# Chunked attention and its feed-forward layer on one core: paired chunks' attention parked in HBM, scale and bias applied to results, differences on VectorE, weight blocks stored later

## The chip, the core and the metric

The program runs on one core of a Trainium2 chip. The core has five engines with a queue each: TensorE (PE, matmuls; its weight loads are shown as PEld), VectorE (DVE), ScalarE (ACT), GpSimd (POOL) and SyncE (SP), whose queue issues every DMA here. The metric is device microseconds of one execution. Three runs of the kernel before gave 628.95, 630.91 and 631.41 us; the median is 630.91 us.

## The reference, cut to what matters

```python
# attention: batch 4, 8 heads, 768 positions, 64 per head; chunks of 32 queries
k_full = concat([mem_k, k[c_start-16 : c_end+8]]);  v_full likewise
scores = 0.125 * q_c @ k_full.T
a = exp(scores - max(scores));  a = a / (sum(a) + 1e-9)
out[c] = a @ v_full
# feed-forward on x = attention as 3072 tokens x 512
h = x @ w_in                     # 512 -> 2048
r = maximum(h, 0)
g = s * (r * r) + b              # s and b are two numbers
y = g @ w_out                    # 2048 -> 512, fp32
```

Since s and b are scalars, `g @ w_out` equals `s * ((r*r) @ w_out) + b * (column sums of w_out)`.

## The kernel before

The 3072 tokens are 8 chunks of 384 (`TOK`). Chunks 0 to 3 take the plain way, chunks 4 to 7 are taken in two pairs, (4,5) and (6,7). fp32 accuracy comes from splitting each operand in a high and a low fp32r part and adding three products.

Plain way: 64 steps, one for each block f of 128 hidden units of a chunk. `hidden` (L572) makes 12 matmuls of 384 columns; ScalarE applies relu, square, scale and bias and writes the high part gH (L580 to L583); VectorE writes the low part gL (L584); `result` (L595) makes 9 matmuls of 512 columns.

Attention comes in 32 visits, four for each chunk, two heads in each (`attend`). A visit is 16 score matmuls (L426), a maximum on VectorE (L494), exponentials on ScalarE (L498), a norm on GpSimd (L507, L510), 8 transposes on VectorE (L530) and 16 value matmuls (L465). For chunks 4 to 7 its result is copied to the ring `words` (L470): four tiles, which the weight loads and the weight blocks use as well.

Weights arrive as 64-bit numbers. 32 of them are put together by ScalarE and VectorE (L547 to L557), and for the pairs `blocks` makes sums of their quarters on GpSimd (L627 to L637), cuts these (L640, L641) and stores the blocks to HBM (L646): 48 stores of 256 KB come from weights as they are (`w1s<-w`, `w2s<-w`), 128 of 128 KB from sums (`<-words`).

A pair uses a seven-product scheme over 2 by 2 blocks. `mix` makes four differences of the attention's blocks on GpSimd (L707) and cuts seven operands (L702, L703). `seven` makes the hidden layer in 8 groups of 42 matmuls (L753), and on each group ScalarE does relu (L785), GpSimd the square (L787) and ScalarE scale and bias (L788). `rest` makes the second layer with 336 matmuls (L855), first taking 32 differences of hidden blocks on GpSimd (L800) and cutting 56 operands (L848 on ScalarE, L849 on VectorE). Weight blocks come back through SP (L731, `word`).

The order on all five engines is laid out when the program is built, by `Plan.lay`: a list planner with a cost for each kind of operation (`HOLD`), a due time for each (`anchor`, `base`), rings with a number of tiles, and a flag `lock` that keeps certain VectorE and GpSimd operations apart in the plan. On the chip each engine then runs its list in order.

Of the kernel before, what the change touches and what calls it, by code (L numbers as in the profile page):

```python
# [11 lines left out]
F32 = mybir.dt.float32  # L12
# [20 lines left out]
TOK = 384  # L33
GB = TOK // QB
# [18 lines left out]
LAST_VISITS = (0.5, 2.6)  # L53
# [19 lines left out]
            low=475, affine_v=475, rec=120, max=212, flip=449, xlow=470, wlow=345, wjoin=610, wsign=612, out=600,  # L73
            small=240, prod=1062, half=527, gsum=1000, add=480, wide=850, square2=1600, vsum=1230, ssum=620, shigh=930, slow=1143, tsum=1700, thigh=670, tlow=880, norm=1010, norm2=2030, wrest=1290, issue=440)
LATE = dict(PE=230, ACT=180, DVE=180, POOL=150, SP=0)
RATE, LAND = 400.0, 2000.0
# [65 lines left out]
class Plan:  # L142
# [25 lines left out]
    def lay(self, filler=None):  # L168
# [18 lines left out]
        while todo:  # L187
# [6 lines left out]
            for e in engines:  # L194
# [78 lines left out]
def body(ctx: ExitStack, tc: tile.TileContext, qkv, w1, w2, out):  # L273
# [3 lines left out]
    w2s = [dram.tile([P, 2, 2, 2 * P], F32, name=f"w2s{i}") for i in range(NWORDS)]  # L277
    plan = Plan()
# [38 lines left out]
    gs = Ring([(const.tile([P, TOK], F32R, name=f"gH{i}"), const.tile([P, TOK], F32R, name=f"gL{i}")) for i in range(3)])  # L317
# [78 lines left out]
    x_vals, open_ = {}, []  # L396

    def attend(ch, c):
# [166 lines left out]
    def hidden(u):  # L565
# [17 lines left out]
        op("ACT", "high", u - ahead, lambda: nc.scalar.activation(g.tile[0], hp(), AF.Copy), (h[0],), (g["H"],))  # L583
        op("DVE", "low", u - ahead, lambda: nc.vector.tensor_tensor(g.tile[1], hp(), g.tile[0].bitcast(F32), ALU.subtract),  # L584
# [35 lines left out]
    def blocks(side, g, due):  # L620
# [22 lines left out]
        for n, name in enumerate(BLOCKS):  # L643
# [8 lines left out]
            else:  # L652
# [3 lines left out]
                put(lambda i=i, k=k: weight_tile(side, fs[i])[:, :, k * 2 * P:(k + 1) * 2 * P].bitcast(F32), dst, parts[i], 0)  # L656
# [20 lines left out]
    cuts = Ring(Lazy([lambda k=k: gs.tiles[k] for k in range(3)] + [lambda s=s: (lambda x: (x[:, 0], x[:, 1]))(again(*s, [P, 2, TOK], F32R)()) for s in spots]))  # L677
# [12 lines left out]
    def mix(ch):  # L690

        due = base(ch) - 6.0
        raw = {name: x_vals[ch + int(name[2]) - 1, int(name[1]) - 1] for name in ("B11", "B12", "B21", "B22")}
        flat = lambda v: v.tile[:, :2 * TOK] if v.ring is words else v.tile.rearrange("p c t -> p (c t)")
        both = lambda v: [v[0], v[1]] if v.ring is words else [v[0]]
# [10 lines left out]
        def subtract(dst, a, b, prio):  # L706
            op("POOL", "tsum", due + prio, lambda: nc.gpsimd.tensor_tensor(flat(dst), flat(a), flat(b), ALU.subtract), [*both(a), *both(b)],  # L707
# [28 lines left out]
    def seven(ch, g):  # L736
# [46 lines left out]
        for v in (gb, ga):  # L783
# [3 lines left out]
            op("POOL", "square2", then, lambda v=v: nc.gpsimd.tensor_tensor(v.tile, v.tile, v.tile, ALU.mult), (), (v[0], v[1]), lock=True)  # L787
            op("ACT", "wide", then, lambda v=v: nc.scalar.activation(v.tile, v.tile, AF.Identity, scale=s_sb, bias=b_sb),  # L788
               (c_s[0], c_b[0]), (v[0], v[1]))

    def rest(ch):

        begin = base(ch) + NF // 2 * GROUP
        here, names = {}, ("P1", "P5", "P2", "P6", "P7", "P3", "P4")
        raw = lambda name, g: (gv[ch + int(name[2]) - 1, g], int(name[1]) - 1)
# [3 lines left out]
        def change(dst, a, b, due):  # L799
            op("POOL", "gsum", due, lambda: nc.gpsimd.tensor_tensor(at(dst), at(a), at(b), ALU.subtract), [part(a), part(b)], [part(dst)], lock=True)  # L800
            return dst

        def operand(name, g, due):
            if name == "P1":
                return raw("B11", g)
            if name == "P5":
                here["T1", g] = change(raw("B11", g), raw("B12", g), raw("B11", g), due - 2.0)
                return here["T1", g]
            if name == "P2":
                return raw("B21", g)  # L810
# [153 lines left out]
```

## Time and profile before

| | before |
|---|---|
| median of 3 runs | 630.91 us |
| the profiled execution | 629.65 us, of which the span is 627.9 us |
| TensorE busy | 602.2 us, 96% |
| VectorE busy | 458.3 us, 73% |
| ScalarE busy | 439.2 us, 70% |
| GpSimd busy | 309.6 us, 49% |
| HBM read, written | 98.57 MB, 35.65 MB |

Busy shares are means over stages with different limits, so they are read by stretch: start-up to about 20 us; weights arrive and are put together until about 121 us; plain steps with attention until about 355 us; the first pair until about 502 us (its `rest` begins at 427 us); the second pair until 624 us; then the last store.

### The profile page before, as it was taken

How to read it: one execution, taken by the hardware profiler on the slowest of the kernel's cores; microseconds unless marked ns; L12 is line 12 of the kernel's file. 1: busy time of each engine (PE TensorE's matmuls, PEld its weight loads, DVE VectorE, ACT ScalarE, POOL GpSimd, SP SyncE). 2: the span in 40 equal slices, each digit the busy share in tenths (PEclk: the TensorE clock that was granted, in tenths of full speed). 3: DMA queues.
4: the chain of work that ended last, by engine and by line, in shares of the span. 5: the costliest groups of instructions: out<-in, count | busy, mean ns of one | idle time of the engine just before them, and what ended most of it. 6: DMA issues, size and time to landing. Idle time of an engine off the chain costs nothing. (4 is left out here: it accounts for less than half of the span.)

```text
span 627.9 us, 11538 instructions
## 1 busy us (share of the span) xinstructions
PE 602.2 (96%) x3822; PEld 539.3 (86%) x3822; DVE 458.3 (73%) x1221; ACT 439.2 (70%) x1127; POOL 309.6 (49%) x290
## 2 busy tenths in 40 slices
PE   9999978999999999999999999999987999999997
PEld 5777867788888888798888999999877899999897
DVE  5999998954767687946777377678997844438874
ACT  6999997867778678659876667888752446656442
POOL 4522100384565687961234065765890526649710
PEclk9999998999999999999999999999997999999999
DMA  9977998425444546345337188777573787777671
GB/s 340 405 269 230 324 355 306 165 72 181 165 160 164 181 150 214 111 150 195 93 98 252 49 273 268 271 259 265 200 234 122 253 286 256 245 255 244 232 256 51
DMA packets 65531, 134.97 MB, mean 215 GB/s; under 512 B 6592, under 2 KB 37312, under 8 KB 65472
## 3 DMA queue, kind: packets, MB, share of 16 engines
q1 hardware_dynamic: 65472, 134.25, 62.7%
q8 instruction: 30, 0.49, 0.3%
q14 instruction: 29, 0.24, 0.1%
HBM read 98.57 MB, written 35.65 MB: 214 GB/s over the span
## 5 line engine op out<-in xcount | busy, mean ns | idle before, releaser
L572 PE MATMUL ps<-x,w 128*128 128x384 f32 x768 | 147.5, 339 | 1.7 <-DVE w L557 1.7
L572 PEld LDWEIGHTS ps<-x,w 128*128 128x128 f32 x768 | 134.8, 188 | 9.6 <-DVE w L557 3.1
L595 PE MATMUL ps<-w,gH 128*128 128x512 f32 x384 | 121.1, 397 | 0.0
L753 PE MATMUL ps<-again,again 128*128 128x384 f32 x672 | 120.3, 338 | 0.0
L753 PEld LDWEIGHTS ps<-again,again 128*128 128x128 f32 x672 | 117.8, 188 | 1.1
L498 ACT ACTIVATE t<-t,nmax 96x128 f32<-96x128 f32 x256 | 99.4, 392 | 18.1 <-DVE nmax L494 18.0
L530 DVE STREAM_TRANSPOSE aT<-t 32x256 f32<-32x256 f32 x192 | 83.6, 435 | 14.3 <-POOL t L510 11.7
L510 POOL TENSOR_TENSOR t<-t,rden 96x1024 f32<-96x1024 f32 (+1 forms) x40 | 66.8, 1672 | 52.8 <-DVE rden L509 52.7
L595 PE MATMUL ps<-w,gL 128*128 128x512 f32 x192 | 79.3, 413 | 9.9 <-DVE gL L584 9.8
L595 PEld LDWEIGHTS ps<-w,gH 128*128 128x128 f32 x384 | 72.8, 190 | 14.4 <-DVE w L557 0.6
L507 POOL TENSOR_SCALAR rden<-den 96x8 f32<-96x8 f32 (+1 forms) x40 | 13.2, 331 | 135.4 <-ACT t L498 134.4
L855 PE MATMUL ps<-gH,again 128*128 128x384 f32 x272 | 69.8, 337 | 0.0
L584 DVE TENSOR_TENSOR gL<-ps,gH 128x384 fp32r<-128x384 f32 x64 | 35.3, 552 | 46.2 <-ACT gH L583 45.6
L494 DVE CUSTOM_DVE_ANT_0 t<-ps,mask 96x128 f32<-96x128 f32 x256 | 57.8, 280 | 9.7 <-PE ps L426 9.4
L580 ACT ACTIVATE ps<-ps 128x384 f32<-128x384 f32 x64 | 30.4, 475 | 43.2 <-PE ps L572 43.1
L595 PEld LDWEIGHTS ps<-w,gL 128*128 128x128 f32 x192 | 36.4, 190 | 21.0 <-DVE gL L584 13.9
L855 PE MATMUL ps<-again,again 128*128 128x384 f32 x264 | 53.1, 348 | 0.0
L855 PE MATMUL ps<-gL,again 128*128 128x384 f32 x136 | 46.9, 345 | 3.6 <-DVE gL L849 3.5
L855 PEld LDWEIGHTS ps<-gH,again 128*128 128x128 f32 x272 | 49.5, 188 | 0.0
L855 PEld LDWEIGHTS ps<-again,again 128*128 128x128 f32 x264 | 47.8, 194 | 1.3 <-DVE again L849 0.8
L498 ACT ACTIVATION_READ_ACCUMULATOR t<-t,nmax 96x1 f32 x256 | 48.6, 190 | 0.0
L627 POOL TENSOR_TENSOR words<-w 128x512 f32<-128x512 f32 x32 | 45.4, 1438 | 0.7
(95 smaller groups left out, 1018.3 us busy)
## 6 DMA issues: line engine op xcount, KB each, us to landing
again<-w1s SPq DMA_DIRECT2D x56, 512.0 KB, 4.2
again<-w2s SPq DMA_DIRECT2D x56, 512.0 KB, 4.2
raw<-qkv SPq DMA_DIRECT2D x28, 448.0 KB, 4.0
words<-w SPq DMA_DIRECT2D x22, 512.0 KB, 5.2
w1s<-words SPq DMA_DIRECT2D x64, 128.0 KB, 1.9
w2s<-words SPq DMA_DIRECT2D x64, 128.0 KB, 1.9
v<-qkv SPq DMA_DIRECT2D x28, 256.0 KB, 3.7
w1s<-w SPq DMA_DIRECT2D x24, 256.0 KB, 4.3
```

What stands on the lines that cost most here:

```text
L494: op("DVE", "max", a + 0.1, lambda j=j: nc.vector.tensor_tensor_reduce(t.tile[:, n, j, :], scv()[:, j, :], mask[:, kind(j)], -SCALE, 3.0e3 ...
L498: op("ACT", "exp", a + 0.2, lambda j=j: nc.scalar.activation(t.tile[:, n, j, :], t.tile[:, n, j, :], AF.Exp, bias=nmax()[:, j:j + 1], scal ...
L507: op("POOL", "small", a + 0.25, lambda: nc.gpsimd.tensor_scalar(rden(), den(), 1e-9, None, ALU.add), [st["d", *x] for x in each], (r,), lo ...
L510: op("POOL", "norm2" if wide else "norm", a + 0.25, lambda: nc.gpsimd.tensor_tensor(t.tile[:, heads], t.tile[:, heads], rden().unsqueeze(3 ...
L530: nc.vector.transpose(aT.tile[gg, :, :, cs], t.tile[cs, :, :, gg])
L572: nc.tensor.matmul(h.tile[:, :TOK], weight_tile(0, f)[:, wi, c * P:(c + 1) * P], x.tile[c][:, xi], start=(c == 0 and n == 0), stop=(c == N ...
L580: op("ACT", "relu", u - ahead, lambda: nc.scalar.activation(hp(), hp(), AF.Relu), (), (h[0],))
L584: op("DVE", "low", u - ahead, lambda: nc.vector.tensor_tensor(g.tile[1], hp(), g.tile[0].bitcast(F32), ALU.subtract), (h[0], g["H"]), (g[" ...
L595: nc.tensor.matmul(acc.tile, g.tile[gi][:, t * P:(t + 1) * P], weight_tile(1, f)[:, wi, :], start=(first and n == 0), stop=(last and n == 2))
L627: op("POOL", "vsum", due, lambda k=k, f=f: nc.gpsimd.tensor_tensor(at(full, 2 * k, 2), weight_tile(side, f)[:, 0].bitcast(F32), weight_til ...
L753: nc.tensor.matmul(bank.tile[:, :TOK], w.tile[:, lo:lo + P], xv.tile[xi][:, kc], start=(not more and kc == 0 and i == 0), stop=(kc == 1 an ...
L855: nc.tensor.matmul(sb(bank), w.tile[:, lo:lo + P], cut.tile[xi], start=(first and k == 0), stop=(last and k == 2), skip_group_check=True)
```

## The change

Five edits. The attention of chunks 4 to 7 is copied to a small tile of another ring and stored to HBM (`xs`, 16 stores of 192 KB); `mix` loads it from there in 8 loads of 384 KB. So visits need no tile of `words`, and their due times run on at one spacing instead of a separate spacing for the last two chunks. In `mix` the differences are taken by VectorE, in `rest` too, except the first eight of each pair, which GpSimd takes right after the group that they need. In `seven` the square moves from GpSimd to ScalarE in the place of scale and bias; s and b act in `rest` on results: the cut operands get two columns more (386), ones in the high part and zeros in the low, so that column 384 of the bank holds the column sums, which ScalarE multiplies by b (`colsum`), and joins multiply by s. The 48 stores of plain weight blocks wait for the last weight (`all_w`). The planner's costs are changed and it knows a delay within one engine (`SAME`).

```diff
 HOLD = dict(...
-            small=240, prod=1062, half=527, gsum=1000, add=480, wide=850, square2=1600, ...
+            small=300, prod=1062, half=525, gsum=985, gsumv=470, tsumv=850, one=180, chigh=420, scaled=400, add=480, wide=735, ...
+SAME = dict(PE=0, ACT=118, DVE=115, POOL=60, SP=0)
...
-        last = (NCHUNK - 2 - NALONE) * (H // 2)
-        if ch < NCHUNK - 2:
-            return VISITS[0] + VISITS[1] * i
-        return base(NCHUNK - 4) + LAST_VISITS[0] + LAST_VISITS[1] * (i - last)
+        return VISITS[0] + VISITS[1] * i
...
-        x = x_vals[ch] if ch < NPLAIN else x_vals[ch, c // 2]
+        x = x_vals[ch] if ch < NPLAIN else Val(wvs, "st")
...
-                op("ACT", "xhigh", due + 0.9, lambda: nc.scalar.activation(x.tile[:, c % 2 * TOK:(c % 2 + 1) * TOK], av(), AF.Copy),
-                   (va[0],), (x[c % 2],))
+                op("ACT", "xhigh", due + 0.9, lambda: nc.scalar.activation(x.tile[:, :TOK], av(), AF.Copy), (va[0],), (x[0],))
+                op("SP", "issue", due + 0.9, lambda: nc.sync.dma_start(xs[ch, c // 2][:, c % 2], x.tile[:, :TOK]), (x[0],),
+                   (c_xs[ch, c // 2][c % 2],), size=P * TOK * 4)
...
-                put(lambda i=i, k=k: weight_tile(side, fs[i])..., dst, parts[i], 0)
+                put(lambda i=i, k=k: weight_tile(side, fs[i])..., dst, [*parts[i], *all_w], 0)
...
-        due = base(ch) - 6.0
+        due = base(ch) - 8.0
+        for name in ("B11", "B12", "B21", "B22"):
+            v, key = Val(words), (ch + int(name[2]) - 1, int(name[1]) - 1)
+            op("SP", "issue", due - 2, lambda v=v, key=key: nc.sync.dma_start(flat(v), xs[key].rearrange("p c t -> p (c t)")), ...)
...
-            op("POOL", "tsum", due + prio, lambda: nc.gpsimd.tensor_tensor(flat(dst), flat(a), flat(b), ALU.subtract), ...
+            op("DVE", "tsumv", due + prio, lambda: nc.vector.tensor_tensor(flat(dst), flat(a), flat(b), ALU.subtract), ...
...
-            op("POOL", "square2", then, lambda v=v: nc.gpsimd.tensor_tensor(v.tile, v.tile, v.tile, ALU.mult), (), (v[0], v[1]), lock=True)
-            op("ACT", "wide", then, lambda v=v: nc.scalar.activation(v.tile, v.tile, AF.Identity, scale=s_sb, bias=b_sb), ...
+            op("ACT", "wide", then, lambda v=v: nc.scalar.activation(v.tile, v.tile, AF.Square), (), (v[0], v[1]))
+        op("POOL", "gsum", then + 1, lambda: nc.gpsimd.tensor_tensor(gb.tile[:, 0], gb.tile[:, 0], ga.tile[:, 0], ALU.subtract), ...)
...
+            if name == "P6":
+                return change("DVE", t1, b22, t1, due - 2.0)
+            if name == "P7":
+                return change("DVE", b11, t1, b11, due - 2.0)
+            if name == "P4":
+                return change("DVE", b21, b21, t1, due - 2.0)
...
+        def colsum(i, bank, due):
+            op("ACT", "one", due, lambda: nc.scalar.activation(col(i), bank.tile[:, TOK:TOK + 1], AF.Identity, scale=b_sb), ...)
+        def join(dst, bank, v, due):
+            op("DVE", "add", due, lambda: nc.vector.scalar_tensor_tensor(sb(dst), sb(bank), s_sb, sb(v), ALU.mult, ALU.add), ...)
...
-                        nc.tensor.matmul(sb(bank), w.tile[:, lo:lo + P], cut.tile[xi], ...
+                        nc.tensor.matmul(sx(bank), w.tile[:, lo:lo + P], cut.tile[xi], ...
```

The first place is the queue of SP while weights arrive. `words<-w` is a weight load, `w1s<-w` and `w2s<-w` are stores of plain weight blocks. Before, a piece of the queue:

```order
L646 DMA w1s_71<-w_8_1051 128x2x256
L646 DMA w1s_73<-w_8_1051 128x2x256
L646 DMA w2s_94<-w_7_1064 128x2x256
L646 DMA w2s_110<-w_7_1064 128x2x256
L545 DMA words_155<-w 128x1024
L545 DMA words_152<-w 128x1024
L646 DMA w1s_74<-w_9_1107 128x2x256
L545 DMA words_153<-w 128x1024
L646 DMA w2s_87<-w_8_1121 128x2x256
L646 DMA w1s_74<-w_10_1132 128x2x256
L646 DMA w1s_76<-w_10_1132 128x2x256
```

Now, the end of the weight loads:

```order
L544 DMA words_160<-w 128x1024
L544 DMA words_161<-w 128x1024
L544 DMA words_162<-w 128x1024
L544 DMA words_163<-w 128x1024
L544 DMA words_160<-w 128x1024
L544 DMA words_161<-w 128x1024
L645 DMA w1s_57<-w_0_468 128x2x256
L645 DMA w1s_59<-w_0_468 128x2x256
L645 DMA w1s_60<-w_1_539 128x2x256
```

All 48 of these stores stood ahead of or among the last weight loads; now all 48 stand behind the last load.

The second place is VectorE in the `rest` of the first pair. `L849` and `L860` are the low cuts, `L530` transposes of a visit, `L835` joins, `L703` and `L707` cuts of the next pair's operands, `L803` a difference. Before:

```order
L849 TENSOR_TENSOR again_7_4242<-againx_3_4229,again_7_4242 128x384
L849 TENSOR_TENSOR gL_171<-again_14_4332,gH_170 128x384
L849 TENSOR_TENSOR gL_173<-again_15_4414,gH_172 128x384
L849 TENSOR_TENSOR gL_175<-againx_0_3753,gH_174 128x384
L530 STREAM_TRANSPOSE aT_163<-t_159 32x8x32 x6
L835 TENSOR_TENSOR wv_150<-ps_179,wv_150 128x384
L835 TENSOR_TENSOR wv_149<-ps_179,wv_149 128x384
L835 TENSOR_TENSOR wv_147<-ps_180,wv_147 128x384
L835 TENSOR_TENSOR wv_148<-ps_180,wv_148 128x384
L530 STREAM_TRANSPOSE aT_163<-t_159 32x8x32 x2
L849 TENSOR_TENSOR again_7_4156<-againx_2_3845,again_7_4156 128x384
```

Now:

```order
L860 TENSOR_TENSOR again_7_4431<-againx_0_3960,again_7_4431 128x384
L860 TENSOR_TENSOR gL_179<-againx_2_4084,gH_178 128x384
L803 TENSOR_TENSOR again_12_4180<-again_12_4161,again_12_4180 128x384
L860 TENSOR_TENSOR gL_181<-again_12_4161,gH_180 128x384
L707 TENSOR_TENSOR again_6_3714<-words_161,again_6_3713 128x768
L860 TENSOR_TENSOR gL_183<-again_13_4265,gH_182 128x384
L803 TENSOR_TENSOR again_13_4277<-again_13_4265,again_13_4277 128x384
L860 TENSOR_TENSOR again_7_4335<-againx_0_4376,again_7_4335 128x384
L803 TENSOR_TENSOR againx_1_4388<-againx_0_4376,againx_1_4388 128x384
L860 TENSOR_TENSOR again_7_4431<-againx_2_4450,again_7_4431 128x384
L803 TENSOR_TENSOR againx_3_4462<-againx_2_4450,againx_3_4462 128x384
```

Transposes and maxima of attention have left this stretch, differences have come in, one for each cut in the last three of the seven products. On TensorE the visits whose values came in the first pair's hidden layer and `rest` (8) become 6, all of them within the hidden layer.

## Rows read from the trace of the kernel before

**Rows 1.** The page's busy times: us, share of the span, instructions.
```profile
PE 602.2 (96%) x3822; PEld 539.3 (86%) x3822; DVE 458.3 (73%) x1221; ACT 439.2 (70%) x1127; POOL 309.6 (49%) x290
```

**Rows 2.** Waits of TensorE: us in all, times, the longest.
```profile
PE ps L595 <- DVE gL L584: 9.8, 7, 3.4
PE ps L465 <- DVE aT L530: 5.5, 3, 4.1
PE ps L855 <- DVE gL L849: 3.5, 3, 1.4
```

**Rows 3.** Stretches: length; PE, PEld, DVE, ACT, POOL busy (instructions); PEclk, DMA share, GB/s.
```profile
20.00:60.00 40.00, 38.74 (x302) 30.42 (x301) 38.37 (x127) 39.67 (x122) 14.92 (x16) 1.00 0.80 285
60.00:120.00 60.00, 51.41 (x265) 43.25 (x266) 55.34 (x118) 50.80 (x111) 2.84 (x5) 0.97 0.91 311
120.00:280.00 160.00, 157.66 (x979) 137.84 (x978) 112.14 (x319) 116.68 (x315) 112.36 (x116) 1.00 0.45 151
280.00:360.00 80.00, 79.74 (x544) 69.88 (x543) 50.89 (x165) 57.85 (x164) 20.23 (x16) 1.00 0.42 140
440.00:500.00 60.00, 52.03 (x316) 48.65 (x315) 53.18 (x112) 32.06 (x82) 38.64 (x28) 0.94 0.60 201
564.00:590.00 26.00, 25.09 (x137) 23.40 (x136) 22.73 (x24) 14.63 (x28) 21.93 (x18) 1.00 0.66 228
```

**Rows 4.** Three shorter stretches, same columns.
```profile
98.00:104.00 6.00, 3.35 (x8) 2.68 (x9) 4.13 (x8) 5.90 (x12) 0.00 (x0) 0.72 0.97 358
460.00:470.00 10.00, 8.72 (x46) 7.52 (x44) 9.74 (x8) 4.60 (x9) 10.00 (x8) 1.00 0.69 226
470.00:480.00 10.00, 5.89 (x29) 5.67 (x30) 7.84 (x16) 1.57 (x3) 2.33 (x3) 0.66 0.28 97
```

**Rows 5.** DMA issues from 28 to 121 us: KB each, median us to landing.
```profile
words<-w SPq DMA_DIRECT2D x18, 512.0 KB, 5.1
w1s<-w SPq DMA_DIRECT2D x23, 256.0 KB, 4.3
w2s<-w SPq DMA_DIRECT2D x22, 256.0 KB, 3.8
```

**Rows 6.** ScalarE's wait for weight loads, 70 to 120 us.
```profile
ACT wv L547 <- DMA words<-w: 4.3, 4, 2.9
```

**Rows 7.** VectorE from 441 to 476 us: start, us, operation.
```profile
441.21 3.58 DVE L530 STREAM_TRANSPOSE aT<-t 32x256 f32<-32x256 f32 x8
...
461.89 5.41 DVE L849 TENSOR_TENSOR gL<-again,gH 128x384 fp32r<-128x384 f32 x2
...
468.51 2.68 DVE L530 STREAM_TRANSPOSE aT<-t 32x256 f32<-32x256 f32 x6
...
475.04 0.55 DVE L849 TENSOR_TENSOR gL<-again,gH 128x384 fp32r<-128x384 f32 x1
```

**Rows 8.** All cuts of `rest` (L849): VectorE's busy time (instructions).
```profile
0.00:628.00 628.00, 85.15 (x112) 0.99 0.63 215
```

**Rows 9.** Groups by line: busy us, mean ns, idle before.
```profile
L494 DVE CUSTOM_DVE_ANT_0 t<-ps,mask 96x128 f32<-96x128 f32 x256 | 57.8, 280 | 9.7 <-PE ps L426 9.4
L703 DVE TENSOR_TENSOR again<-words,again 128x768 fp32r<-128x768 f32 x14 | 19.7, 1420 | 1.7 <-ACT again L702 1.5
L785 ACT ACTIVATE again<-again 128x768 f32<-128x768 f32 x8 | 6.8, 845 | 6.4 <-DVE again L779 6.4
L788 ACT ACTIVATE again<-again,b_sb,s_sb 128x768 f32<-128x768 f32 x16 | 16.4, 1026 | 5.4 <-POOL again L787 5.3
```

**Rows 10.** A cut of `mix` alone, and one beside GpSimd.
```profile
480.56 0.95 DVE L703 TENSOR_TENSOR again<-words,again 128x768 fp32r<-128x768 f32 x1
493.16 2.61 DVE L703 TENSOR_TENSOR again<-words,again 128x768 fp32r<-128x768 f32 x1
```

**Rows 11.** GpSimd's norm, by form.
```profile
L510 POOL TENSOR_TENSOR t<-t,rden 96x1024 f32<-96x1024 f32 x24 | 47.9, 1994 | 39.9 <-DVE rden L509 39.8
```

**Rows 12.** TensorE from 520 to 560 us, by line.
```profile
L753 PE MATMUL ps<-again,again 128*128 128x384 f32 x229 | 40.4, 337 | 0.0
```

More of the change, by code (lines that the diff above doesn't have):

```diff
@@ L72 @@
             relu=388, square=388, affine=570, high=388, xhigh=388, wscale=571, whigh=536, copy=270, exp=386, keep=388, store=480, bias=500,
[L73 to L74 removed]
+            low=475, affine_v=475, rec=120, max=212, flip=449, xlow=470, wlow=365, wjoin=610, wsign=612, out=600,
+            small=300, prod=1062, half=525, gsum=985, gsumv=470, tsumv=850, one=180, chigh=420, scaled=400, add=480, wide=735, vsum=1260, ssum=700, shigh=950, slow=1143, tsum=1800, thigh=735, tlow=880, norm=1010, norm2=1870, wrest=1290, issue=440)
 LATE = dict(PE=230, ACT=180, DVE=180, POOL=150, SP=0)
+SAME = dict(PE=0, ACT=118, DVE=115, POOL=60, SP=0)
 RATE, LAND = 400.0, 2000.0
@@ L253, in lay @@
                     d.left -= 1
-                    d.ready = max(d.ready, free[e] if d.eng == e and not o.size else o.end)
+                    d.ready = max(d.ready, free[e] + SAME[e] if d.eng == e and not o.size else o.end)
                     if not d.left:
@@ L277, in body @@
     w2s = [dram.tile([P, 2, 2, 2 * P], F32, name=f"w2s{i}") for i in range(NWORDS)]
+    xs = {(ch, i): dram.tile([P, 2, TOK], F32, name=f"xs{ch}_{i}") for ch in range(NPLAIN, NCHUNK) for i in range(NC_T // 2)}
     plan = Plan()
@@ L396, in body @@
     x_vals, open_ = {}, []
+    c_xs = {key: fixed() for key in xs}
     def attend(ch, c):
@@ L676, in body @@
     spots = [(0, 7), (1, 7)]
-    cuts = Ring(Lazy([lambda k=k: gs.tiles[k] for k in range(3)] + [lambda s=s: (lambda x: (x[:, 0], x[:, 1]))(again(*s, [P, 2, TOK], F32R)()) for s in spots]))
+    cuts = Ring(Lazy([lambda k=k: gs.tiles[k] for k in range(3)] + [lambda s=s: (lambda x: (x[:, 0], x[:, 1]))(again(*s, [P, 2, TOKX], F32R)()) for s in spots]))
     streams, stream_slots = later([(k, f) for f in range(8, 12) for k in range(2)], [P, 2 * DM], F32R)
@@ L801, in change @@
             return dst
         def operand(name, g, due):
[L804 to L810, printed above, removed]
+            b11, b21, t1, b22 = (gv[ch, g], 0), (gv[ch, g], 1), (gv[ch + 1, g], 0), (gv[ch + 1, g], 1)
             if name == "P6":
-                here["T2", g] = change(here["T1", g], raw("B22", g), here["T1", g], due - 2.0)
-                return here["T2", g]
+                return change("DVE", t1, b22, t1, due - 2.0)
@@ L847, in rest @@
                 gone = first("cut", [(4, k) for k in range(3)] + spots)
-                op("ACT", "high", due - AHEAD, lambda cut=cut, v=v: nc.scalar.activation(cut.tile[0], at(v), AF.Copy), (part(v),), [cut["H"], *gone])
-                op("DVE", "low", due - AHEAD, lambda cut=cut, v=v: nc.vector.tensor_tensor(cut.tile[1], at(v), cut.tile[0].bitcast(F32), ALU.subtract),
-                   (part(v), cut["H"]), [cut["L"], *gone], lock=True)
+                op("ACT", "chigh", due - AHEAD, lambda cut=cut, v=v: nc.scalar.activation(cut.tile[0][:, :TOK], at(v), AF.Copy), (part(v),), [cut["H"], *gone])
+                op("DVE", "low", due - AHEAD, lambda cut=cut, v=v: nc.vector.tensor_tensor(
+                    cut.tile[1][:, :TOK], at(v), cut.tile[0][:, :TOK].bitcast(F32), ALU.subtract), (part(v), cut["H"]), [cut["L"], *gone], lock=True)
+                ends = []
+                if gone:
+                    for k in range(2):
+                        ends.append(cut["end", k])
+                        op("ACT", "one", due - AHEAD - 1, lambda cut=cut, k=k: nc.scalar.activation(
+                            cut.tile[k][:, TOK:], ones[:, :TOKX - TOK], AF.Copy, scale=1.0 - k), (), [ends[k], *gone])
                 def products(bank, m, w, cut, first, last, q):
@@ L854, in products @@
                         lo = q * DM + wi * 2 * P + m * P
-                        nc.tensor.matmul(sb(bank), w.tile[:, lo:lo + P], cut.tile[xi], start=(first and k == 0), stop=(last and k == 2),
+                        nc.tensor.matmul(sx(bank), w.tile[:, lo:lo + P], cut.tile[xi], start=(first and k == 0), stop=(last and k == 2),
                                          skip_group_check=True)
@@ L859, in rest @@
                     op("PE", "half", due, lambda m=m, w=w, cut=cut, g=g, i=i, bank=banks_[m], more=more: products(
-                        bank, m, w, cut, g == 0 and not more, g == NF // 2 - 1, i % 2), (w[0], cut["H"], cut["L"]), (banks_[m][0],))
+                        bank, m, w, cut, g == 0 and not more, g == NF // 2 - 1, i % 2), (w[0], cut["H"], cut["L"], *ends), (banks_[m][0],))
             due -= AHEAD
@@ L912, in body @@
         result(u)
+    for ch in range(NPLAIN, NCHUNK):
+        visits(ch)
     for ch in range(NPLAIN, NCHUNK, 2):
-        visits(ch)
-        visits(ch + 1)
         mix(ch)
```

80 lines of the change are left out of this document (45 added, 35 removed).

## The prediction

> **What bounds the kernel now.** I read first the page's busy times: TensorE works 602.2 us, 96% of the span of 627.9 us [rows 1], so at most 25.7 us are to be had from its idle time, and no edit takes matmuls away. The next view is TensorE's waits: VectorE ends nearly all of them, 9.8 us before second-layer matmuls of the plain way, 5.5 us before value matmuls, 3.5 us in `rest` [rows 2]. The stretches say where. TensorE's idle time is the length less its busy time [rows 3]: 1.3 us from 20 to 60 us, 8.6 from 60 to 120, 2.3 from 120 to 280, 0.3 from 280 to 360, 8.0 from 440 to 500, 0.9 from 564 to 590. The reader is to see two holes, one while weights arrive and one in the first pair's `rest`, and almost nothing between. After both holes the clock falls to the lower of its two levels, 1.2 GHz, for a part of the stretch: 0.72 over 6 us and 0.66 over 10 us [rows 4], worth 6 x 0.28 = 1.7 us and 10 x 0.34 = 3.4 us of work at full rate. TensorE stood idle before and within both.
>
> In the first hole two things are late together. VectorE is busy 55.3 of 60 us, so it is nearly the bound itself, but it idles 4.7 us there and 1.6 us from 20 to 60 [rows 3], and ScalarE, which feeds it, waits 4.3 us for weight loads [rows 6]. DMA is 0.91 busy at 311 GB/s, and among 18 loads of 512 KB stand 45 stores of 256 KB: 11.5 MB of stores beside 9.2 MB of weights [rows 5]. In the second hole VectorE is busy 53.2 of 60 us [rows 3], but with slow instructions: two cuts take 5.41 us where one alone takes 0.55 [rows 7], in a stretch in which GpSimd is busy 10.00 of 10 us [rows 4]. Behind them stand the transposes for which the value matmuls wait up to 4.1 us [rows 2, 7].
>
> **The change part by part.**
>
> Stores later. The stores leave the weight phase; 9.2 MB of weights and few other loads remain for 93 us, about half of the wire at the rate measured. DMA is then no longer late; VectorE is next, and its work is the same. So the phase can shorten by VectorE's idle time, 1.6 + 4.7 = 6.3 us, and not by more unless its idle time before 20 us shrinks too. I take 5 us: some idle time will remain as ScalarE's waiting for TensorE. Bounds: 0, if ScalarE and VectorE wait for each other just as long without DMA, and 11.6, if TensorE's whole 9.9 us and the clock's 1.7 come back. The stores now run from some 115 us on, 12.6 MB at 311 GB/s = 40 us, in a stretch where DMA is 0.45 busy [rows 3]. Behind them on SP wait the first loads of later visits; those of the next visits stand ahead of the last weight loads, so I cost this at nothing. Without that cover a visit comes late, and a plain step does not depend on one.
>
> Attention earlier. By the order four visits' VectorE work leaves the first pair for the plain stage. One is 8 transposes, 3.6 us [rows 7], and 8 maxima of 0.28 us at most [rows 9], 5.8 us with them; four make 23 us. The plain stage from 120 to 360 us has 47.9 + 29.1 = 77 us of idle VectorE and 65.5 of idle ScalarE [rows 3], so the visits fit; their matmuls only change place. Yet at 2.6 us of idle in 240 there is nothing to gain, and denser visits can cost a stall here and there. I take +1.5 us; bounds -1 and +6 (the 5.5 us of waits for transposes once more [rows 2]). The way through HBM adds a store of 192 KB and a load of 384 KB, each a matter of 4 to 5 us to landing like those of [rows 5]; `mix` is due eight steps before its use, over 30 us, which hides it.
>
> The second hole. `rest` of the first pair loses visits' VectorE work and GpSimd's norms, differences and `mix`. What is left on VectorE, counted in the order: 51 cuts, 24 differences, 12 joins, 87 instructions of about 0.55 us = 48 us, and 5 operations of `mix` at 0.95 [rows 10] = 5 us. TensorE's 336 matmuls follow each other in 40/229 = 0.175 us [rows 12], 58.7 us. VectorE stays below, at 53. The 0.55 holds only if GpSimd no longer slows the cuts: 112 of them took 85.2 us, 0.76 each, against 0.55 alone [rows 7, 8], so 23 us of VectorE's time was standing still. GpSimd keeps eight differences a pair, all laid before `rest`. So the 8.0 us of idle and the 3.4 of the low clock go except for a stall where `rest` begins, as in the second pair (0.9). I take -9; bounds -4 and -11.4.
>
> The second pair. Its 0.9 us in `rest` mostly goes: -0.7; bounds -0.9 and +2, since VectorE gains 24 differences there.
>
> Square on ScalarE. It takes the place of the affine: 0.85 for 1.03 us, if a square costs what relu costs [rows 9], and GpSimd's square drops out of the chain. ScalarE is half idle there, so nothing. Column sums and the added biases are some 10 short instructions a pair on the same idle engine; the multiply by s lies in a join that runs anyway.
>
> Two columns more. 672 matmuls of 386 columns for 384: 0.175 x 2/384 = 0.9 ns each, +0.6 us; below it nothing, above it 1 us.
>
> The sum goes by the profiled execution, 629.65 us: 629.65 - 5 + 1.5 - 9 - 0.7 + 0.6 = 617.05. The median of the runs stands 1.26 us above that execution, so 618.3: I say 618 us.
>
> A rule that speaks against taking differences on VectorE. The trace shows the cuts of `mix`, which read two SBUF tiles, at 0.95 us alone, at 2.61 beside GpSimd and at 1.42 in the mean [rows 9, 10]. By the mean, four differences in the plain stage lose 4 x 0.47 = 1.9 us of VectorE, which its idle time hides. The Trainium skill, "SBUF — State Buffer", section "Who interferes with whom", says that a VectorE instruction with two SBUF inputs and a GpSimd one that reads SBUF block each other for a whole instruction. By that rule each of the four could lose a norm of 1.99 us [rows 11], 8 us in all, and if TensorE waited for all of it the sum would be 617.05 - 1.5 + 8 = 623.6. The mean of the 14 cuts speaks for the smaller price.
>
> **The rivals.**
>
> Load phase no shorter (B). VectorE at 55.3 of 60 us is the bound and the stores were hidden. For it: VectorE is fuller than DMA at 0.91 [rows 3]; against it: ScalarE's waits for loads [rows 6]. 617.05 + 5 + 1.26 = 623.3 us.
>
> Everything comes back (D). Both holes and both low clocks vanish, 11.6 + 11.4 + 0.9, plain stage unharmed: 629.65 - 23.9 + 0.6 + 1.26 = 607.6 us. Against it: VectorE stays at over nine tenths of the weight phase.
>
> Denser visits stall the plain steps (C). The order scores 18 visits in the plain stage after the weights. TensorE's ten waits for VectorE in the plain way and for transposes lasted 9.8 + 5.5 us [rows 2], 1.5 each; if every one of the 18 visits costs half of that, 0.7 us, the plain stage pays 12.6 in place of 1.5: 618.3 + 11.1 = 629.4 us, no change. Against it: VectorE's 77 us of idle time.
>
> VectorE becomes the bound of `rest`, slower (E). If its 87 instructions went on at the 0.76 us of [rows 8], 66 us, plus 5, they would stand over TensorE's 58.7 by 12 us in the first pair, and by 7 in the second, which has no `mix`: 618.3 + 19 = 637.3 us. It decides once an instruction takes (58.7 - 5)/87 = 0.62 us in the first pair; slower than before from about 0.73. For it: more of VectorE's instructions there read SBUF alone. Against it: GpSimd has nothing left to do in `rest`.
>
> **How the numbers follow.** Forecast 0.58, B 0.12, D 0.15, C 0.08, E 0.07. Within 0.5% (3.2 us) is about what a measurement can tell from no change. Faster: forecast, B and D, 0.85; same: C, 0.08; slower: E, 0.07. The likeliest's own range is 613 to 623 (load phase -2 to -7, first pair -6 to -11, plain stage 0 to +4); to hold eight in ten with B and most of D it goes from 609 to 626 us.
>
> **What would show it.** Right: from 60 to 120 us no wait of ScalarE for loads, VectorE over 57 of 60 us, the last weight joined some 5 us before 121; TensorE idle under 3 us in the first pair and the clock at its full level there; cuts of `rest` at a mean near 0.55 us and GpSimd empty in it; idle time of TensorE in the plain stage under 5 us. Wrong: weights joined no earlier (B); value matmuls waiting for transposes in the plain stage (C); TensorE waiting for cuts through all of `rest` (E).

## The result and the profile after

The changed kernel takes 621.18 us (median of 4 runs, 620.30 to 622.08) where the kernel before takes 630.33 (4 runs, 628.95 to 631.41): a ratio of 0.9856, 95% interval 0.9827 to 0.9885. That is 9.2 us less. The forecast was 618 us, by its terms 12.6 us less than the kernel before. The profiled execution took 620.3 us with a span of 618.5 us. Its busy times, as in [rows 1]:

```profile
PE 598.8 (97%) x3832; PEld 541.4 (88%) x3832; DVE 447.2 (72%) x1277; ACT 437.2 (71%) x1157; POOL 184.6 (30%) x202
```

GpSimd lost 125 us of work and VectorE, which took over most of its differences, lost 11. The same stretches as [rows 3], and three of 20 us (columns as there):

```profile
20.00:60.00 40.00, 39.99 (x313) 32.10 (x312) 39.24 (x133) 40.00 (x127) 14.48 (x17) 1.00 0.56 208
60.00:120.00 60.00, 55.08 (x285) 46.61 (x283) 55.83 (x130) 52.61 (x124) 8.91 (x10) 0.97 0.70 247
120.00:180.00 60.00, 52.26 (x313) 45.65 (x312) 31.00 (x81) 35.17 (x85) 36.01 (x39) 0.91 0.75 252
120.00:280.00 160.00, 151.46 (x985) 132.85 (x984) 105.82 (x338) 114.07 (x323) 105.32 (x112) 0.97 0.62 204
140.00:160.00 20.00, 14.94 (x121) 12.93 (x119) 5.45 (x22) 9.74 (x29) 8.82 (x10) 0.93 0.97 319
160.00:180.00 20.00, 18.48 (x100) 16.07 (x101) 15.10 (x42) 13.70 (x37) 11.40 (x13) 0.82 0.55 185
280.00:360.00 80.00, 78.79 (x546) 68.36 (x545) 55.59 (x197) 59.79 (x185) 18.06 (x17) 1.00 0.55 187
440.00:500.00 60.00, 60.00 (x341) 60.00 (x340) 49.58 (x96) 35.67 (x72) 1.02 (x1) 1.00 0.82 268
564.00:590.00 26.00, 26.00 (x150) 26.00 (x149) 23.21 (x48) 15.49 (x33) 0.00 (x0) 1.00 0.81 262
```

Read length less TensorE's busy time against before. Weight phase (20 to 120 us): 9.85 us idle before, 4.93 now. First pair's `rest`: 7.97 before, none now, and the clock, 0.94 before, is full. Second pair: 0.91 before, none now. But from 120 to 280 us 2.34 became 8.54, and the clock fell from 1.00 to 0.97 there. A new hole has come, and the 20 us rows place it: about 155 us, with DMA 0.97 busy from 140 to 160 us and the clock at 0.82 behind it. Two of TensorE's waits over the whole run, as in [rows 2]:

```profile
PE ps L594 <- DVE gL L583: 12.8, 6, 6.6
PE ps L463 <- DVE aT L529: 0.8, 1, 0.8
```

The one for transposes has nearly gone; of the other, one wait makes half. TensorE's timeline (start, us, operation, in brackets the idle time before and its releaser) shows it:

```profile
153.82 1.12 PE L426 MATMUL ps<-raw 64*96 64x128 f32 x16
161.52 0.79 PE L594 MATMUL ps<-w,gL 128*128 128x512 f32 x1 [6.58 <-DVE gL L583]
```

`gL` is VectorE's low part of a plain step, which had stood in the way before too [rows 2], but for 3.4 us at most. VectorE waited in turn for ScalarE, whose timeline is:

```profile
150.91 0.47 ACT L472 ACTIVATE x<-ps 128x384 fp32r<-128x384 f32 x1
151.28 0.47 ACT L580 ACTIVATE ps<-ps 128x384 f32<-128x384 f32 x1
158.24 1.06 ACT L639 ACTIVATE words<-words 128x1024 fp32r<-128x1024 f32 x1 [6.48 <-DMA w1s<-words]
159.20 0.63 ACT L581 ACTIVATE ps<-ps,b_sb,s_sb 128x384 f32<-128x384 f32 x1
159.86 0.49 ACT L582 ACTIVATE gH<-ps 128x384 fp32r<-128x384 f32 x1
```

The square (L580) of the step was done at 151.75. Its scale and bias (L581) needed nothing but ScalarE, but the cut of a sum (L639) stood ahead of it in ScalarE's list and waited 6.48 us for a tile of `words` that a store of earlier sums still held. Why that store was late stands in SP's queue (start, us, operation):

```profile
105.01 14.29 SPq L645 DMA_DIRECT2D w1s<-w  x19
...
131.46 6.79 SPq L645 DMA_DIRECT2D w2s<-w  x10
138.36 3.90 SPq L645 DMA_DIRECT2D w1s<-words  x8
142.30 6.64 SPq L645 DMA_DIRECT2D w2s<-w  x10
149.04 2.37 SPq L645 DMA_DIRECT2D w1s<-words  x4
...
152.46 1.95 SPq L645 DMA_DIRECT2D w1s<-words  x4
```

The deferred stores (`<-w`) go out as one burst, and the stores of the sums (`<-words`), on which tiles of the ring depend, stand between them. The chain that ends ScalarE's wait runs through one of these (start, us):

```profile
152.94 0.43 SPq L645
153.41 4.75 DMA w1s<-words
```

This store of 128 KB was issued behind 44 of the 48 plain ones, and took 4.75 us to land; the median of such stores from 105 to 160 us is 2.6 us here, and 2.0 in the run e2_spread below, where the other stores are spread.

The account closes by the first matmul of each stage. Up to the first pair: 354.9 before, 367.5 now, +12.6. First pair's hidden layer: 71.9 to 69.5, -2.4. From its `rest` to the second pair: 75.0 to 59.3, -15.7. Second pair: 61.1 to 59.1 and 61.1 to 59.1, -4.0. In all -9.5, and the span shrank by 9.4.

Part of the first two numbers is work that only changed its place: 29 batches of score matmuls and 27 of value matmuls now stand ahead of the first pair, 24 and 24 before. At 1.12 and 0.88 us a batch that is 5 x 1.12 + 3 x 0.88, about 8 us. (By the order six visits kept their values in the pair; on the chip one of the six came at 365.6 us, just ahead of it.) Without it the stretch up to the first pair lost about 4 us, and the first pair gained about 10.

### The profile page after: what moved, and what is told of

The parts are those of the page before. It is cut to its first block, busy times and chain, and to the rows that moved or that the text cites. A ratio compares the mean times of both kernels' runs of the same rounds, so it can differ in the third digit from the quotient of the medians.

```text
span 618.5 us, 11572 instructions
## 1 busy us (share of the span) xinstructions
PE 598.8 (97%) x3832; PEld 541.4 (88%) x3832; DVE 447.2 (72%) x1277; ACT 437.2 (71%) x1157; POOL 184.6 (30%) x202
## 4 chain that ended last, share of the span: by engine, by line
PE 60%; ACT 16%; DVE 9%; POOL 5%; DMA 4%; issue 3%; SPq 2%; DVEq 0%; ACTq 0%; POOLq 0%
PE ps L757 19%; PE ps L872 19%; PE ps L594 8%; PE ps L571 7%; ACT t L497 6%; DVE aT L529 3%; PE ps L426 2%; POOL t L509 2%; SPq L645 2%; PE ps L463 2%; ACT ps L581 2%; DMA words<-w 2%; DVE gL L583 2%; ACT wv L546 2%; ACT ps L579 1%
## 5 line engine op out<-in xcount | busy, mean ns | idle before, releaser
L594 PE MATMUL ps<-w,gH 128*128 128x512 f32 x384 | 123.1, 402 | 0.2 <-DVE w L556 0.2
L757 PE MATMUL ps<-again,again 128*128 128x384 f32 x672 | 120.1, 338 | 0.0
L497 ACT ACTIVATE t<-t,nmax 96x128 f32<-96x128 f32 x256 | 100.8, 399 | 22.8 <-DVE nmax L493 22.3
L594 PE MATMUL ps<-w,gL 128*128 128x512 f32 x192 | 80.0, 416 | 13.0 <-DVE gL L583 12.8
L872 PE MATMUL ps<-gH,again 128*128 128x386 f32 x272 | 70.2, 339 | 0.0
L493 DVE CUSTOM_DVE_ANT_0 t<-ps,mask 96x128 f32<-96x128 f32 x256 | 58.6, 281 | 13.3 <-PE ps L426 13.1
L506 POOL TENSOR_SCALAR rden<-den 96x8 f32<-96x8 f32 (+1 forms) x40 | 11.8, 295 | 151.1 <-ACT t L497 150.2
L497 ACT ACTIVATION_READ_ACCUMULATOR t<-t,nmax 96x1 f32 x256 | 50.6, 198 | 0.0
L872 PE MATMUL ps<-again,again 128*128 128x386 f32 x264 | 50.1, 338 | 0.0
L872 PE MATMUL ps<-gL,again 128*128 128x386 f32 x136 | 46.0, 339 | 0.0
L626 POOL TENSOR_TENSOR words<-w 128x512 f32<-128x512 f32 x32 | 41.6, 1314 | 4.5 <-DMA w1s<-words 3.5
```

Source lines behind the costliest of these rows:

```text
L493: op("DVE", "max", a + 0.1, lambda j=j: nc.vector.tensor_tensor_reduce(t.tile[:, n, j, :], scv()[:, j, :], mask[:, kind(j)], -SCALE, 3.0e3 ...
L497: op("ACT", "exp", a + 0.2, lambda j=j: nc.scalar.activation(t.tile[:, n, j, :], t.tile[:, n, j, :], AF.Exp, bias=nmax()[:, j:j + 1], scal ...
L594: nc.tensor.matmul(acc.tile, g.tile[gi][:, t * P:(t + 1) * P], weight_tile(1, f)[:, wi, :], start=(first and n == 0), stop=(last and n == 2))
L626: op("POOL", "vsum", due, lambda k=k, f=f: nc.gpsimd.tensor_tensor(at(full, 2 * k, 2), weight_tile(side, f)[:, 0].bitcast(F32), weight_til ...
L757: nc.tensor.matmul(bank.tile[:, :TOK], w.tile[:, lo:lo + P], xv.tile[xi][:, kc], start=(not more and kc == 0 and i == 0), stop=(kc == 1 an ...
L872: nc.tensor.matmul(sx(bank), w.tile[:, lo:lo + P], cut.tile[xi], start=(first and k == 0), stop=(last and k == 2), skip_group_check=True)
```

## The experiments

Theory 1: the 48 later stores cost their gain again, by the stall at 155 us. Its rival, theory 2: the denser visits made that stall, and the stores are harmless. Theory A: the hole in `rest` went because VectorE's cuts and GpSimd's differences no longer hold each other up. Its rival, theory B: because the visits left that stretch. For the kernel before, the runs on the same chips gave 630.3 to 630.5 us.

**e1_early: the changed kernel with the stores as early as before.**

```diff
-  put(..., dst, [*parts[i], *all_w], 0)
+  put(..., dst, parts[i], 0)
```

> The changed kernel with one part undone: the 48 stores of plain weight blocks wait for their own weight alone, so they stand among the weight loads again. Theory 1 (the burst of these stores after the weight phase holds up the sums' stores, so tiles of the words ring come free late, ScalarE stands at its cut of the sums and TensorE idles 6.65 us at 154.7 us, then runs at the low clock): idle time of TensorE from 120 to 280 us falls from 8.5 to about 2.5 us and the clock there is 1.00; the weights are joined about 5 us later (121 for 115.5 us) and idle time from 20 to 120 us rises from 4.9 to about 9 us; 617 us. Theory 2 (the stall comes from the denser visits or from the new users of the rings, the stores are harmless): the stall near 155 us stays and the weight phase is longer, 625 us.

Measured 621.23 us (ratio 0.9849, 0.9826 to 0.9872).

```profile
60.00:120.00 60.00, 47.17 (x247) 38.46 (x246) 49.38 (x104) 45.52 (x101) 2.91 (x4) 1.00 0.89 301
120.00:180.00 60.00, 58.36 (x356) 51.11 (x355) 39.12 (x110) 42.81 (x110) 44.36 (x44) 1.00 0.43 141
```

The rows are stretches, as in [rows 3]; so are all rows below that begin with a range of time. From 120 to 180 us the stall is gone with the burst (1.6 us idle for 7.7), but the weight phase stands idle for 12.8 us in place of 4.9, and the last weight is joined at 123.0 in place of 115.5. Both kernels take 621.2. Theory 1 has the stall right and the time wrong, 617 us: it put the idle time from 20 to 120 us at 9 us, and 13.1 was measured. In the changed kernel the edit that was to shorten the weight phase brings nothing: it moves the loss to 155 us.

**e2_spread: the same stores, released in groups.** Each waits for the cut of the sums to which its block belongs, where it had waited for the last weight.

```diff
+  tok = fixed()
-  op("ACT", "shigh", due, ..., every, (high[0],))
+  op("ACT", "shigh", due, ..., every, (high[0], tok[0]))
-  put(..., dst, [*parts[i], *all_w], 0)
+  put(..., dst, [*parts[i], tok[0]], 0)
```

> The changed kernel with the 48 stores kept out of the weight phase and out of one burst: each waits for ScalarE's cut of the sums of its own block group, three stores a group. Theory 1 (the burst made the stall): the weight phase stays as short as in the changed kernel (last join near 115.5 us), idle time of TensorE from 120 to 280 us falls from 8.5 to about 2.5 us and the low clock there goes; 612 us. Theory 2 (the stall comes from the denser visits or the rings): 621 us with the stall still there.

Measured 614.82 us (0.9746, 0.9720 to 0.9773).

```profile
60.00:120.00 60.00, 54.00 (x288) 45.96 (x286) 57.65 (x133) 53.89 (x128) 10.00 (x10) 1.00 0.51 171
120.00:180.00 60.00, 57.91 (x366) 50.75 (x368) 36.68 (x101) 40.59 (x106) 38.54 (x41) 1.00 0.69 227
```

The weight phase keeps most of its gain (6.3 us idle from 20 to 120 us, the last weight joined at 117.0), the idle time from 120 to 180 us shrinks to 2.1 us, and the clock stays full: 6.4 us less than the changed kernel, though 2.8 more than theory 1 said. Theory 2 is out, since the visits' spacing is as there. And from 120 to 165 us TensorE makes two visits' scores and two visits' values in the kernel before, in the changed one and in this one alike: where the stall came, the visits were no denser. Run again on another chip:

> The changed kernel with the stores spread, again, beside the run above on the same chip: 614.8 us as measured. It says which of the two versions is the faster; a difference under 0.5% counts as none.

614.79 us (0.976, 0.974 to 0.978). No version that was run is faster by more than the noise.

**e3_before_later: the kernel before, with its stores after the last weight.** The diff is that of e1_early, turned round.

> The kernel before with one part of the change alone: the 48 stores wait for the last weight. Theory 1: the weight phase gets about 5 us shorter, and a stall of 5 to 10 us with a low clock comes between 130 and 180 us; the second hole stays; 630 to 635 us, no gain. Theory 2 (stores later is a gain by itself, the stall needs the new attention path): no stall over 2 us between 120 and 180 us, 625 us.

Measured 628.32 us (10 runs; 0.9968, 0.9954 to 0.9982).

```profile
120.00:180.00 60.00, 59.32 (x371) 51.46 (x369) 35.25 (x107) 41.67 (x112) 34.57 (x39) 1.00 0.81 270
145.00:165.00 20.00, 19.60 (x118) 16.77 (x118) 14.41 (x52) 14.10 (x44) 8.73 (x9) 1.00 1.02 332
```

DMA is as full as in the changed kernel, and TensorE is idle for 0.7 us from 120 to 180 us. Neither theory's time is met (630 to 635, and 625 us): by itself the edit gains 2.0 us. Theory 1 in its simple form falls: a burst alone makes no stall. ScalarE did wait for a store here,

```profile
ACT words L640 <- DMA w1s<-words: 4.0, 1, 4.0
```

but no matmul waited for what stood behind: the plain step at hand had been finished ahead of the cut. So, as far as these two orders show, it takes the burst and an order in which a sum's cut stands on ScalarE's list ahead of operations of a plain step that TensorE needs next.

**e6_rate: the changed kernel, whose planner is told of a slower wire.** The burst stays and the cuts are laid elsewhere, but the whole order is laid anew: the first pair begins at 349.1 us instead of 367.5, with two more visits' values in it.

```diff
-RATE, LAND = 400.0, 2000.0
+RATE, LAND = 300.0, 2000.0
```

> The changed kernel with one constant of its planner altered: the wire is laid out at 300 bytes per ns instead of 400, so the plan knows of later landings; the 48 stores stay one burst. Theory 1' (the stall at 154.7 us comes from the burst together with the place of the sums' cut on ScalarE's list, which the plan put too early for the wire as it is): the burst stays (DMA share over 0.8 from 120 to 160 us), the cut stands later and the stall of 6.65 us shrinks to under 2 us, with the clock at 1.00; 613 to 616 us. Theory 1 (the burst alone makes it): a stall of 5 us or more stays between 140 and 170 us; 621 us.

Measured 617.37 us (0.9795, 0.9767 to 0.9823).

```profile
120.00:180.00 60.00, 56.07 (x377) 48.89 (x378) 37.63 (x124) 41.88 (x119) 34.30 (x37) 1.00 0.77 255
```

As many bytes as in the changed kernel, and half of its idle time: 3.9 us. TensorE's waits for a `gL` in the whole run:

```profile
PE ps L594 <- DVE gL L583: 11.5, 10, 2.6
```

The longest was 2.6 us for 6.6, where theory 1' had said under 2, and 3.8 of the 6.4 us that spreading gives came back, against 5 to 8 forecast. With e3_before_later this is the second order in which the same burst does less harm.

**e7_spread_rate: both edits.**

> The kernel with the stores spread over their block groups, with the same altered constant. Theory 1 (the spread already took the whole stall away): nothing more to gain, 614 to 616 us. Theory 1': with the stores spread the wire is half empty and the plan's rate matters little; the same 614 to 616 us. Faster than 613 us would show that late landings cost elsewhere too, in the weight phase above all.

615.12 us (0.9759, 0.9732 to 0.9785), no different from e2_spread. The same new order that gained 3.8 us with the burst gains nothing without it, so its gain was the burst's stall, and not the rest of the order: the two edits remove one and the same stall.

**e4_pool: the changed kernel with the differences back on GpSimd.** Four differences of `mix`, and in `rest` those of P6, P7 and P4.

```diff
-  op("DVE", "tsumv", due + prio, lambda: nc.vector.tensor_tensor(...
+  op("POOL", "tsum", due + prio, lambda: nc.gpsimd.tensor_tensor(...
-  return change("DVE", t1, b22, t1, due - 2.0)
+  return change("POOL", t1, b22, t1, due - 2.0)
```

> The changed kernel with one part undone: the differences of mix and those for P6, P7 and P4 in rest are GpSimd's again (all but the first eight of a pair). Theory A (GpSimd beside VectorE's cuts made the second hole): cuts of rest rise from a mean near 0.55 to 0.7 us or more, TensorE idles 3 to 8 us in the two rests together, 625 us. Theory B (the attention that left this stretch made the hole, GpSimd is harmless without it): cuts may be slow, but TensorE idles under 1.5 us in both rests; 621 us.

Measured 636.88 us (1.0096, 1.0065 to 1.0126): 15.7 us more than the changed kernel, slower than before, and 12 us over theory A's figure. The first pair's `rest` took 70.2 us instead of 59.3, the second pair's 62.8 instead of 59.1. The hole is back in the stretch that the visits have left:

```profile
440.00:500.00 60.00, 53.31 (x280) 48.16 (x280) 52.96 (x60) 33.47 (x66) 38.34 (x28) 1.00 0.69 221
```

VectorE's and GpSimd's timelines show how (start, us, operation):

```profile
466.83 1.36 DVE L860 TENSOR_TENSOR again<-againx,again 128x384 fp32r<-128x384 f32 x1
468.12 1.36 DVE L860 TENSOR_TENSOR gL<-againx,gH 128x384 fp32r<-128x384 f32 x1
469.40 1.37 DVE L860 TENSOR_TENSOR gL<-again,gH 128x384 fp32r<-128x384 f32 x1
```

```profile
466.45 2.61 POOL L803 TENSOR_TENSOR again<-again,again 128x384 f32<-128x384 f32 x2
469.02 2.62 POOL L803 TENSOR_TENSOR againx<-againx,againx 128x384 f32<-128x384 f32 x2
```

One cut for each difference, both at a step of 1.3 us. The 112 cuts took 95.7 us, 0.85 each, against 0.76 before [rows 8] and 0.56 in the changed kernel. The rows of this run and of the changed kernel (whole span, VectorE's busy time in the cuts of `rest`, clock, DMA share, GB/s):

```profile
0.00:650.00 650.00, 95.71 (x112) 0.99 0.66 217
0.00:650.00 650.00, 62.89 (x112) 0.99 0.64 217
```

**e8_before_dve: the kernel before, with its differences on VectorE.** Nothing else: the visits stay where they were, and so does the square.

```diff
-  op("POOL", "tsum", due + prio, lambda: nc.gpsimd.tensor_tensor(...
+  op("DVE", "tlow", due + prio, lambda: nc.vector.tensor_tensor(...
-  op("POOL", "gsum", due, lambda: nc.gpsimd.tensor_tensor(...
+  op("DVE", "low", due, lambda: nc.vector.tensor_tensor(...
```

> The kernel before with one part of the change alone: the differences of mix and rest on VectorE, all else as before (visits in the first pair, square on GpSimd, scale and bias per group). Theory A (GpSimd beside the cuts made the second hole): cuts of rest fall from 0.76 to 0.6 us or less, TensorE idles 2 to 4 us instead of 8.0 from 440 to 500 us, 622 us. Theory B (the visits made it): VectorE has 36 more instructions a pair on top of the visits, the hole stays at 8 us or grows, 631 us or more.

Measured 619.89 us (0.9839, 0.9818 to 0.9861): this one edit gains as much as the whole change. The first pair's `rest`, and then all of its cuts on VectorE:

```profile
440.00:500.00 60.00, 58.40 (x375) 56.87 (x373) 58.23 (x138) 35.22 (x89) 11.73 (x8) 1.00 0.75 242
```

```profile
0.00:650.00 650.00, 65.11 (x112) 1.00 0.63 208
```

VectorE has more to do than before (58.2 of 60 us), with all visits' transposes still there, and TensorE's idle time fell from 8.0 to 1.6 us. Theory A holds, and B isn't needed for this gain. The cuts gave 20 us of VectorE's time back (85.15 to 65.11). How much of the gain is that and how much that a difference itself takes 0.55 us on VectorE and 1.02 on GpSimd, no run separates.

**e10_dve_spread: e8 with the spread stores of e2.**

> The kernel before with two parts: differences on VectorE, and the 48 stores spread over their block groups. If the two gains add up: 619.9 less the shorter weight phase (the run with the spread won 6.4 us on the changed kernel, of which the weight phase's part is 3 to 5) = 615 to 617 us, no stall near 155 us. If the spread's gain belongs to the changed kernel's plan alone: 619 us or more.

616.97 us (0.9782, 0.9754 to 0.9810), 2.9 us under e8 and at the upper end of 615 to 617: a gain by the stores comes on top, but it is the weight phase's, since e8 has no stall to lose. On the same chip e2b_spread took 614.79, 0.35% less, under the 0.5% that counts as a difference here. So with both parts in, the attention by HBM, the square on ScalarE and s and b on results make 2.2 us together, no more than the noise.

**e5_visits and e9_visits_flush: the changed kernel with the last two chunks' visits as late as before.** e5 restores their due times:

```diff
+  if ch < NCHUNK - 2:
+      return VISITS[0] + VISITS[1] * i
+  return base(NCHUNK - 4) + LAST_VISITS[0] + LAST_VISITS[1] * (i - last)
```

> The changed kernel with one part undone: the last two chunks' visits are due at the separate spacing of the kernel before (from the first pair's start on), their results still go by HBM and differences stay on VectorE. Theory A (GpSimd beside VectorE's cuts made the second hole, the visits alone do not): cuts of rest stay near 0.55 us but for those beside the norms, TensorE idles under 3 us in the first pair; 622 us. Theory B (the visits in rest made the hole): TensorE idles 5 us or more in the first pair's rest, waiting for transposes or cuts; 628 us.

646.35 us (1.0257, 1.0227 to 1.0287). It is no clean undo: the last values of chunk 5 now waited for visits of chunk 6, and TensorE stood for 5.7 us at values and 4.7 us at the hidden layer between 360 and 380 us. e9 restores the condition that keeps these apart:

```diff
-  if ch + 1 < NCHUNK:
+  if ch + 1 not in (NCHUNK - 2, NCHUNK):
```

> The run with the old spacing of the last visits once more, this time with the end of chunk 5 as in the kernel before: its last two visits no longer wait for the first of chunk 6. So it is the changed kernel with the last eight visits in the first pair, eight values there and in rest as before. Theory A (GpSimd beside the cuts made the second hole, visits in rest are harmless): TensorE idles under 3 us from 360 us to the second pair, 621 to 623 us. Theory B (visits in rest cost by themselves): 5 us or more of idle time there, 627 us.

633.54 us (1.0048, 1.0032 to 1.0064), 12.4 us over the changed kernel.

```profile
440.00:500.00 60.00, 49.79 (x298) 47.17 (x297) 56.29 (x135) 34.55 (x89) 5.21 (x4) 0.91 0.66 216
```

By its time and its idle time this is theory B's case. The hole of 10.2 us is there with GpSimd nearly idle and the cuts at 0.58 us each, so GpSimd does not explain it. TensorE's waits for cuts:

```profile
PE ps L876 <- DVE again L864: 4.8, 2, 3.8
PE ps L876 <- DVE gL L864: 3.8, 3, 2.2
```

VectorE, from 478 us:

```profile
478.30 0.96 DVE L715 TENSOR_TENSOR words<-words,words 128x768 f32<-128x768 f32 x1
479.17 0.96 DVE L711 TENSOR_TENSOR again<-words,again 128x768 fp32r<-128x768 f32 x1
480.04 0.96 DVE L715 TENSOR_TENSOR words<-words,words 128x768 f32<-128x768 f32 x1
480.91 0.96 DVE L711 TENSOR_TENSOR again<-words,again 128x768 fp32r<-128x768 f32 x1
481.78 0.96 DVE L715 TENSOR_TENSOR words<-words,words 128x768 f32<-128x768 f32 x1
```

These are `mix` of the second pair. It can begin only when the late visits have come back from HBM (ScalarE waited 2.1 us for such a load), and its differences and cuts stand here nearly in one row in front of a cut that `rest` needs, for which TensorE waited 2.2 us. In front of the cut of the longest wait, 3.8 us, stood a late visit's transposes (3.58 us from 465.30), four joins (2.19 us) and three operations of `mix`. TensorE waited 8.6 us for cuts in all. So in the changed kernel the earlier attention is worth something. In e8, which has no way through HBM, TensorE's whole idle time in that stretch is 1.6 us with the visits late and about as many transposes and operations of `mix` in it (24 and 10, for 23 and 10). How much of the 12.4 us is the way through HBM and how much the other order that the planner then chose, no run separates.

## Why the prediction was right, and where its size was off

Faster was right, and so was the mechanism of both gains. The time lies 3.2 us above the forecast, because one step failed: the later stores, "in a stretch where DMA is 0.45 busy", of which it said "I cost this at nothing". That step cost 6.4 us; that the time is only 3.2 us off is luck, since the second hole and the second pair gave more than their terms.

- **Stores later, weight phase, -5.** The size came out: 4.9 us of idle time went, and the last weight was joined at 115.5, 5.6 us earlier. But the term hangs on the order. The same edit alone took 2.2 us of this idle time in the order before (9.85 to 7.62, e3_before_later) and 8.1 in the changed order (13.07 in e1_early to 4.93), so that the two kernels differ by 4.9 is in part luck. VectorE was to be over 57 of 60 us: it is at 55.8 here, but at 58.6 in e3_before_later and 57.7 in e2_spread, so it is the next bound, as said. ScalarE still waits for loads, 1.7 us where 4.3 stood [rows 6].
- **The same stores, afterwards, 0. This is the step that failed.** Behind them I looked for visits' loads and found cover. What stood among them was the stores of the sums, and their tiles of `words` were waited for at the head of ScalarE's list. I had written "a plain step does not depend on one", of visits; by ScalarE's order it depended on a sum's cut. The idle time grew by 6.2 us from 120 to 280 us, and the sign named in the forecast, under 5 us of idle time in the plain stage, failed. The clock, 0.97 for 1.00 over 151 us of work, cost up to 4.5 us more by that row; the account leaves less, since of the 4 us lost up to the first pair 2.8 are idle time (13.2 to 16.0). The price in time is what spreading brought back: 6.4 us (e2_spread, e2b_spread).
- **Attention earlier, +1.5.** Outside that stall the plain stage idles 0.6 us more: 8.54 - 6.58 = 1.96 us from 120 to 280 us, where 2.34 stood before, and 1.21 from 280 to 360, where 0.26 did. TensorE's waits for transposes in all of the run fell from 5.5 us [rows 2] to 0.8. Nothing of rival C. The visits' matmuls that moved there, about 8 us, are paid back in the first pair.
- **The second hole, -9.** Too small: all 8.0 us of idle time and the clock's 0.06 x 60 = 3.6 us came back, about the lower bound of that term. The account agrees: about 10 us in the first pair, and 2 in the second pair's hidden layer (next point). From its first matmul to the second pair `rest` takes 59.3 us, 336 matmuls without a gap, with VectorE busy for 50.4 us of it (53 forecast). The reason was the right one (e4_pool, e8_before_dve), the cuts fell to 0.56, and GpSimd has 1.0 us of work from 440 to 500 us. I had kept back a stall at its start as in the second pair; none came. VectorE after 441 us, where before a batch of transposes and pairs of slow cuts stood [rows 7]:

```profile
447.30 0.55 DVE L860 TENSOR_TENSOR gL<-againx,gH 128x384 fp32r<-128x384 f32 x1
447.76 0.55 DVE L860 TENSOR_TENSOR again<-againx,again 128x384 fp32r<-128x384 f32 x1
448.23 1.02 DVE L803 TENSOR_TENSOR againx<-againx 128x384 f32<-128x384 f32 x2
449.17 0.55 DVE L860 TENSOR_TENSOR again<-again,again 128x384 fp32r<-128x384 f32 x1
```

- **The second pair, -0.7.** It gained 2.0 us in `rest`, of which 0.9 is the idle time of [rows 3]. The 2.0 us of its hidden layer are no gain of its own: 12 matmuls of the first `rest` stood in that stretch before, and none now.
- **Two columns more, +0.6; the square on ScalarE, 0.** The 336 matmuls of 386 columns in a `rest` take 59.3 us in the first pair and 59.1 in the second; the 336 of 384 columns in the second pair's hidden layer take 59.1. So the first cost 0.2 us a pair at most. No wait of TensorE names the square or `colsum`.
- **The rivals.** B is out (the phase is shorter), E too (no cut is waited for in `rest`). D's price was right for the second hole; of the first, 4.9 of 11.6 us came back. The rival that came was not among them: a stall of plain steps by their order behind a DMA.

The rule that spoke against taking differences on VectorE was weighed and priced small. The trace agrees with it where the two engines do meet: in e4_pool a cut of 0.55 us takes 1.36 for as long as GpSimd has differences, one for one. (The Trainium skill, "SBUF — State Buffer", "Who interferes with whom": VectorE's second port is GpSimd's too, and is held by one of them for an instruction.) The measured step of 1.3 us is less than the two whole instructions in turn would make, 0.55 + 1.02 = 1.57 us. In the changed kernel they hardly meet: the 14 cuts of `mix` take 0.95 us each, where they took 1.42 [rows 9], so neither price of the rule, 1.9 or 8 us, was paid.

## What to carry to other kernels

A transfer that is put off needs two looks at its new place: the wire's busy share there, and which tiles the transfers beside it hold, with the place of whoever waits for these tiles on its in-order engine. Here it paid to release such transfers in groups, by an event that paces them, rather than all by one late event. Where two-input VectorE work and GpSimd work meet on SBUF in a stretch that feeds TensorE, moving GpSimd's part onto VectorE can make VectorE's part ready earlier, although it has more to do. And a term measured in one order of the engines' lists need not hold in another: the same edit of the stores took 2.2 us of idle time from the weight phase in one and 8.1 in the other.

## What the runs showed of the hardware that was not expected

- VectorE and GpSimd fall into step: a 128x384 cut takes 1.36 us where alone it takes 0.55, and each of GpSimd's differences 1.3 us beside it where alone it takes 1.02 (e4_pool; alone: changed kernel). Neither shows a wait; only the duration tells.
- A full wire need not be a stall: DMA at 1.02 over 20 us left TensorE 0.4 us of idle time (e3_before_later), and at 0.97 over 20 us 5.1 us (changed kernel).
- TensorE's clock fell to a mean of 0.82 over the 20 us behind the gap of 6.58 us, part of it at the lower level; with waits of at most 1.6 us in e2_spread and 2.6 in e6_rate it stayed at 1.00 from 120 to 180 us.
